# Batch 0 of an attention and gated-MLP kernel on a path of its own: k loaded channel by channel, q, x and u in two halves of the positions, in a new order of all steps

## The chip, the cores and the metric

The program runs on one core of one Trainium2 chip. Its engines work at the same time, each through its own stream of instructions: TensorE (PE in the profile; PEld is its weight load), VectorE (DVE), ScalarE (ACT), GpSimd (POOL) and SyncE (SP), which here only issues transfers. The metric is the time of one execution in device microseconds; a smaller number is better. Three runs of the kernel before gave 516.26, 516.77 and 518.28 us.

## The reference, cut to what matters

There are 8 batches, 8 heads, 576 positions and 64 channels per head. q gets a softmax over its channels, k one over its positions; k and v make a 64x64 matrix per head, q times it is x. x (576 x 512 per batch) goes through a gated MLP whose second half is mixed over the positions.

```python
q_s = softmax(q, axis=-1)                 # over 64 channels, 1e-9 in the sum
k_s = softmax(k, axis=2)                  # over 576 positions
kv  = einsum('bhsd,bhse->bhde', k_s, v)
x   = einsum('bhsd,bhde->bhse', q_s, kv)  # as (8, 576, 512)
h   = gelu_tanh(x @ w_in)                 # 512 -> 1024
u, v = h[..., :512], h[..., 512:]
v_n = (v - mean(v)) / sqrt(var(v) + 1e-6) * g_ln
v_s = einsum('ts,bsd->btd', w_sg, v_n) + b_sg[None, :, None]
out = x + (u * v_s) @ w_out
```

## The kernel before

**Steps.** All work is cut into small steps, each a function of the kernel that issues one or a few instructions (`q_max b h`, `hu_mm b f`). The text `PLAN` (line 31 on) lists some 1,400 of them by hand; the loop at line 698 calls them in that order. The class `InOrder` (line 139) chains what each of DVE, ACT, POOL and SP gets, so that every engine works strictly in the order of the plan; `mm` (line 234) does the same for PE. All four have one line in the profile, L148, and PE has L235. Between engines an instruction waits for its operands and for its buffer. All transfers are issued by SP, in the plan's order too.

**Numbers in a step's name.** The first is the batch. For q, k, kv and x the second is the half of the heads (four heads, 256 channels); for q_turn, x_high and x_low it is a pair of heads (128 channels, 0 to 3). For hu it is a block of 128 columns of the u half of w_in, for hv a tile of 128 positions. A V, A or G behind a step names the engine that it is put on.

**q.** `load_q` brings one half of the heads with channels in two groups of 32 partitions. The steps are q_max (DVE, the largest of 32 channels: 128 x 1152 to 128 x 36), q_swapm (four ACT copies of 32 partitions, which exchange the results of the two groups), q_top (DVE, the larger of both), q_sub (POOL or DVE), q_exp (ACT), q_sum, q_swapd, q_inv, q_mul (the same once more for the sum) and q_turn (DVE, a transpose in 32 x 32 pieces that gives channels on the partitions, buffers `qt`).

**k.** `load_k` brings positions on the partitions. k_ma, k_mb and k_mc (DVE) take the maximum over five tiles of positions, kt_mm (PE) transposes it, k_top (DVE) ends it, kb_mm (PE) spreads it back, k_sub (DVE, 128 x 1280) subtracts it from `kk`, k_exp is on ACT. kv_mm makes 20 products of `kk` and `vv` (a column of ones gives the sum), kv_inv and kv_scale divide into `kvt`.

**x and the MLP.** x_mm makes x on PE; x_high (ACT) rounds it to a 32-bit format that PE takes at full rate, x_low (DVE, or x_neg on PE and a copy on ACT) keeps the rest. hu_mm makes three sums of products (high by high, high by low, low by high) for one block of u, hv_mm the same for one tile of v. hv_mm 0 1 is the first product with positions as rows, and needs all of batch 0's x and four blocks of w_in. The rest (gelu, statistics, hv_norm, sg_mm, gate, out_mm, out_add, out_rest, out_store) is the same in all batches.

**Weights.** w_in and w_out come as 64-bit numbers, read as two 32-bit words. For each block of w_in wi_a (ACT) and wi_b, wi_c, wi_d (DVE, buffers `ot_i`) put the two words together, wi_h (ACT) rounds, and the rest is wi_l, on DVE, on POOL, or on PE and ACT (wi_x). hu needs blocks 0 to 3, hv blocks 4 to 7.

**Buffers.** Accumulators are three double banks (`ps2`: x, u, gate, out) and two single ones (`ps1`: kt, kb, kv, hv, wx), each taken in turn. q, k and v have two slots each (one per half of the heads), u five, `gh` and `o` four.

Of the kernel before, what the change touches and what calls it, by code (L numbers as in the profile page):

```python
# [34 lines left out]
q_top 0 1, k_sub 0 0, q_sub 0 1, wi_a 6, q_sum 0 0, q_exp 0 1, wi_b 6, k_ma 0 1, ws_h 0, wi_c 6, q_swapd 0 0, ws_x 0, k_mb 0 1, wi_d 6, ws_h 2
k_mc 0 1, q_inv 0 0, k_exp 0 0, q_sum 0 1, wi_l 1, kt_mm 0 1, wi_a 4, kv_mm 0 0, k_top 0 1, q_swapd 0 1, wi_b 4, q_mul 0 0 1 V, kb_mm 0 1, wi_h 6
load_k 1 0, ws_l 0 A, q_inv 0 1, wi_c 4, ws_h 1, kv_inv 0 0, k_sub 0 1, load_w_sg 4, q_mul 0 0 0, load_v 0 1, ws_h 3, load_w_out 0, load_g
q_mul 0 1 1, wi_a 7, k_exp 0 1, q_mul 0 1 0, q_turn 0 0, q_turn 0 1, kv_scale 0 0, load_q 1 0, q_turn 0 3, x_mm 0 0, wi_a 5, k_ma 1 0, ws_h 4, wi_b 5
q_turn 0 2, b_h, kv_mm 0 1, x_high 0 0, wi_d 4, k_mb 1 0, x_high 0 1, x_neg 0 0, load_v 1 0, load_k 1 1, wi_b 7, wi_c 5, wi_c 7, wi_x 6, wi_h 4
load_w_out 3, kv_inv 0 1, load_q 1 1, load_w_out 1, k_mc 1 0, x_low 0 0 A, x_neg 0 1, kv_scale 0 1, wi_d 5, wi_l 6 A, kt_mm 1 0, x_mm 0 1, k_top 1 0  # L40
wi_h 5, wi_d 7, load_w_out 2, x_low 0 1 A, kb_mm 1 0, q_max 1 0, wi_x 5, b_l, wi_l 4, x_high 0 3, x_high 0 2, x_low 0 3, q_swapm 1 0, x_low 0 2
k_sub 1 0, wi_h 7, wo_a 0, wi_l 5 A, wi_l 7 V, hu_mm 0 0, hu_mm 0 2, k_ma 1 1, wo_a 3, wo_b 0, k_exp 1 0, k_mb 1 1, wo_c 0, wo_b 3, wo_a 1, k_mc 1 1
q_top 1 0, wo_c 3, kt_mm 1 1, kv_mm 1 0, k_top 1 1, q_sub 1 0, q_max 1 1, kb_mm 1 1, hu_mm 0 1, load_v 2 0, load_v 1 1, q_swapm 1 1, kv_inv 1 0
kv_scale 1 0, wo_d 0, q_exp 1 0, q_top 1 1, k_sub 1 1, q_sub 1 1, wo_a 2, q_sum 1 0, hv_mm 0 1, k_exp 1 1, wo_b 2, wo_d 3, wo_b 1, q_swapd 1 0
q_exp 1 1, hv_mm 0 3, hv_gelu 0 1, wo_c 2, q_inv 1 0, wo_c 1, q_mul 1 0 0 V, q_sum 1 1, q_mul 1 0 1, hv_gelu 0 3, hv_mm 0 0, wo_d 2, q_swapd 1 1
q_turn 1 0, wo_h 2, q_inv 1 1, wo_d 1, hu_gelu 0 0, kv_mm 1 1, q_turn 1 1, q_mul 1 1 1, hu_gelu 0 2, hv_stat 0 1, hv_gelu 0 0 A, load_q 2 0
q_mul 1 1 0, x_mm 1 0, load_v 2 1, load_k 2 1, q_turn 1 3, ws_l 3, hv_mm 0 2, load_k 2 0, x_high 1 0, x_high 1 1, kv_inv 1 1, q_turn 1 2, kv_scale 1 1
x_low 1 0, load_q 2 1, hu_gelu 0 1, hv_pow 0 1, x_low 1 1, hv_sq 0 0, hv_norm 0 1, x_mm 1 1, q_max 2 0, ws_l 4, hu_mm 0 3, x_high 1 3, hv_stat 0 0 A
x_high 1 2, hv_pow 0 0, hv_gelu 0 2 A, x_low 1 3, hv_stat 0 3, hv_high 0 1, x_low 1 2, hv_pow 0 3, wo_h 3, wo_h 1, hv_mm 0 4, hv_sq 0 2, hv_low 0 1
hv_norm 0 3, ws_l 1 V, hv_high 0 3, q_swapm 2 0, hv_mm 1 1, hv_gelu 0 4 A, hv_sq 0 4, k_ma 2 0, hv_stat 0 2 A, hv_norm 0 0, k_mb 2 0, k_ma 2 1  # L50
k_mc 2 0, hv_high 0 0, hv_low 0 3, hv_pow 0 2, hv_mm 1 3, hu_gelu 0 3, q_top 2 0, hv_gelu 1 1 A, k_mb 2 1, ws_l 2 V, hv_stat 0 4 A, hv_norm 0 4
hv_pow 0 4, hv_sq 1 1, hv_norm 0 2, hv_low 0 0, hv_high 0 2, hv_mm 1 2, q_sub 2 0 V, hv_low 0 2, hv_gelu 1 3, tail_high 0, tail_again 0, tail_low 0
tail_high 1, k_mc 2 1, sg_mm 0 1, hv_gelu 1 2 A, q_max 2 1, q_exp 2 0, gate 0 1, q_swapm 2 1, hv_sq 1 2, kt_mm 2 0, kt_mm 2 1, sg_mm 0 0, k_top 2 0
tail_low 1, q_sum 2 0, q_swapd 2 0, q_top 2 1, hv_stat 1 3, wo_l 1, kb_mm 2 0, k_top 2 1, sg_mm 0 3, k_sub 2 0, q_sub 2 1, hv_stat 1 2 A, gate 0 0
k_exp 2 0, hv_pow 1 3, gate_high 0 1, q_exp 2 1, kv_mm 2 0, sg_mm 0 2, q_inv 2 0, hv_norm 1 2, hv_norm 1 3, q_mul 2 0 0 V, q_mul 2 0 1, gate_high 0 0
wo_l 2, q_sum 2 1, gate 0 3, gate_high 0 3, q_turn 2 0, wo_l 3 V, hv_mm 1 0, gate_low 0 0, q_swapd 2 1, load_k 3 0, gate 0 2, gate_low 0 1
gate_high 0 2, kv_inv 2 0, q_turn 2 1, kv_scale 2 0, wo_h 0, gate_low 0 2 G, load_q 3 0, gate_low 0 3, out_mm 0 2, wo_l 0, hv_gelu 1 0 A, kb_mm 2 1
k_sub 2 1, k_ma 3 0, out_mm 0 0, tail_again 1, hv_sq 1 0, out_add 0 2, k_mb 3 0, q_max 3 0, q_swapm 3 0, k_exp 2 1, hv_stat 1 0 A, q_inv 2 1
out_add 0 0, q_mul 2 1 0, hv_pow 1 0, q_top 3 0, hv_norm 1 0, out_mm 0 3, out_mm 0 1, q_sub 3 0 V, k_mc 3 0, out_add 0 1, out_rest 0 0 V, q_exp 3 0
kt_mm 3 0, out_rest 0 1, hu_mm 1 0, k_top 3 0, q_mul 2 1 1 V, out_add 0 3, q_sum 3 0, q_turn 2 3, hv_stat 1 1 A, kb_mm 3 0, kv_mm 2 1, hu_gelu 1 0  # L60
hv_pow 1 2, out_rest 0 2, out_rest 0 3 V, hv_pow 1 1, x_mm 2 0, load_v 3 1, out_store 0 1, hu_mm 1 3, out_store 0 3, x_high 2 0, load_k 3 1
hv_high 1 2, x_high 2 1, x_low 2 0, hv_norm 1 1, q_swapd 3 0, hv_high 1 3, hv_low 1 2, hv_high 1 0, hu_mm 1 2, hv_high 1 1, hv_low 1 3, hv_low 1 0
x_low 2 1, hu_mm 1 1, hu_gelu 1 2, hv_low 1 1, q_turn 2 2, load_q 3 1, hu_gelu 1 3, out_store 0 0, q_inv 3 0, k_sub 3 0, q_mul 3 0 0, k_ma 3 1
sg_mm 1 0, k_mb 3 1, k_mc 3 1, sg_mm 1 1, kt_mm 3 1, q_mul 3 0 1 V, q_turn 3 0, q_turn 3 1, load_v 3 0, load_q 4 0, out_store 0 2, q_max 3 1
kv_inv 2 1, q_swapm 3 1, kv_scale 2 1, hu_gelu 1 1, q_top 3 1, gate 1 0, k_exp 3 0, q_sub 3 1, sg_mm 1 2, k_top 3 1, q_max 4 0, gate_high 1 0
gate 1 1, q_swapm 4 0, gate_low 1 0 G, q_exp 3 1, kb_mm 3 1, sg_mm 1 3, gate 1 2, gate_high 1 1, q_top 4 0, q_sum 3 1, q_sub 4 0, k_sub 3 1
q_swapd 3 1, gate_low 1 1 G, k_exp 3 1, x_mm 2 1, gate 1 3, q_inv 3 1, kv_mm 3 0, gate_high 1 2, q_mul 3 1 1 V, gate_high 1 3, q_mul 3 1 0 V
kv_mm 3 1, x_high 2 2, x_high 2 3, q_turn 3 2, q_exp 4 0, load_k 4 1, gate_low 1 2, load_v 4 1, gate_low 1 3, out_mm 1 3, x_low 2 2, out_mm 1 2
kv_inv 3 0, q_turn 3 3, load_q 4 1, kv_scale 3 0, x_low 2 3, load_v 4 0, load_k 4 0, q_sum 4 0, out_add 1 3, hv_mm 2 1, q_max 4 1, out_add 1 2
out_mm 1 0, hv_gelu 2 1 A, out_rest 1 2, out_rest 1 3 V, q_swapd 4 0, k_ma 4 1, out_store 1 3, out_mm 1 1, hv_sq 2 1, out_add 1 0, q_swapm 4 1  # L70
hv_stat 2 1 A, kv_inv 3 1, hv_pow 2 1, q_top 4 1, k_ma 4 0, kv_scale 3 1, q_sub 4 1 V, x_mm 3 0, q_inv 4 0, hv_mm 2 0, q_exp 4 1, k_mb 4 0
out_add 1 1, q_mul 4 0 1, k_mb 4 1, out_rest 1 0, x_high 3 1, hv_mm 2 3, hv_gelu 2 0, out_rest 1 1 V, out_store 1 1, out_store 1 2, x_high 3 0
hv_stat 2 0, hu_mm 2 0, hv_gelu 2 3 A, hv_norm 2 0, hv_pow 2 0, q_turn 4 1, k_mc 4 1, x_low 3 0, hv_norm 2 1, hv_mm 2 2, hu_gelu 2 0, x_low 3 1
hv_sq 2 3, q_sum 4 1, k_mc 4 0, q_mul 4 0 0 V, x_mm 3 1, hu_mm 2 2, x_high 3 2, q_swapd 4 1, x_low 3 2, q_turn 4 0, hv_gelu 2 2 A, q_inv 4 1
# [673 lines left out]
```

## Time and profile before

| What | Value |
|---|---|
| Median of three runs | 516.77 us (516.26 to 518.28) |
| Span of the profiled execution | 515.9 us |
| First operation on PE | between 10 and 20 us |
| Last product on PE begins | 510.50 us |
| Last addition on DVE begins | 512.72 us |
| POOL's first operation with two operands | 15.16 us |
| Table loads on ACT | 24, 1283 ns each |

The page lists the busy time of each engine over the span, then the span in 40 slices of 12.9 us with the busy tenths of each. The table of stretches gives the same for chosen stretches, in us. A timeline row has the start, the duration, the engine, the line, the operation, and what it makes of what, with the number of like instructions that follow one another; in square brackets stands how long the engine was idle before, and which engine or transfer released it. A row of waits has the total, the number and the longest. In a row of the grouped lines the mean in ns follows the busy time. All of them come from the one profiled execution.

### The profile page before, as it was taken

To read this page: it belongs to the slowest core of one execution; us is meant where nothing else is said; L and a number is where in the kernel's file an instruction comes from. 1 tells how busy PE (TensorE), PEld (TensorE's weight loads), DVE (VectorE), ACT (ScalarE), POOL (GpSimd) and SP (SyncE) were. 2 spreads that over 40 slices of the span, in tenths; PEclk is the share of its full clock that TensorE was granted. 3 is DMA by queue.
4 is the path that set the end of the run, shared out by engine and by line. 5 is a ranking of instruction groups with operands and counts; after the bars stand their busy time and mean duration, and the time that the engine had idled before them with its cause. 6 is when DMAs were issued, how large, how long until landed. Compare 5 with 4: busy or idle time off the path is not lost.

```text
span 515.9 us, 9312 instructions
## 1 busy us (share of the span) xinstructions
PE 488.9 (95%) x3846; PEld 446.2 (86%) x3846; DVE 352.9 (68%) x597; ACT 251.1 (49%) x491; POOL 136.2 (26%) x110
## 2 busy tenths in 40 slices
PE   1659999999999999999999999999999999999996
...
DVE  6998999988887966688477866635654462266124
...
GB/s 316 361 266 243 103 246 1 53 46 99 241 10 267 48 87 6 2 75 55 192 89 56 51 243 47 1 90 118 93 1 1 55 39 1 1 0 93 1 1 91
DMA packets 19053, 48.86 MB, mean 95 GB/s; under 512 B 1602, under 2 KB 8132, under 8 KB 19012
## 3 DMA queue, kind: packets, MB, share of 16 engines
...
q8 instruction: 30, 0.49, 0.4%
q14 instruction: 11, 0.09, 0.1%
...
## 4 chain that ended last, share of the span: by engine, by line
PE 86%; DVE 9%; DMA 3%; ACT 1%; issue 1%; POOL 0%; SPq 0%
PE ps L235 86%; DMA qq<-q 2%; DVE ot_i L148 1%; DMA raw_vnh<-w_in 1%; DVE qd L148 1%; DVE kk L148 1%; DVE qm L148 1%; DVE qt L148 1%; DVE ulow L148 1%; DVE u L148 1%; DVE km L148 1%; DVE qq L148 0%; DVE o L148 0%; DVE v L148 0%; POOL ulow L148 0%
## 5 line engine op out<-in xcount | busy, mean ns | idle before, releaser
L148 POOL TENSOR_TENSOR rs<-ve,half 128x1 f32<-128x1 f32 x36 | 28.4, 788 | 113.0 <-DVE ve L148 111.7
L235 PE MATMUL ps<-ulow,wo_h 128*128 128x288 f32 x256 | 55.6, 296 | 0.9 <-DVE ulow L148 0.8
L148 DVE TENSOR_TENSOR u<-ps,u 128x576 f32<-128x576 f32 x32 | 24.0, 754 | 46.5 <-PE ps L235 41.7
L235 PE MATMUL ps<-ws_h,vnh 128*128 128x288 f32 x256 | 55.6, 299 | 0.1
L235 PE MATMUL ps<-gh,wo_h 128*128 128x288 f32 x256 | 55.7, 296 | 0.0
L235 PE MATMUL ps<-gh,wo_l 128*128 128x288 f32 x256 | 55.2, 294 | 0.0
L235 PE MATMUL ps<-ws_h,vnl 128*128 128x288 f32 x256 | 54.7, 295 | 0.0
L235 PE MATMUL ps<-ws_l,vnh 128*128 128x288 f32 x256 | 54.5, 294 | 0.0
L148 ACT CAST gh<-u 128x576 fp32r<-128x576 f32 x32 | 21.0, 670 | 57.4 <-DVE u L148 57.3
L148 POOL TENSOR_TENSOR qq<-qq,qm 128x1152 f32<-128x1152 f32 x12 | 26.1, 2176 | 78.5 <-DVE qm L148 54.4
L148 POOL TENSOR_TENSOR ulow<-u,gh 128x576 fp32r<-128x576 f32 x16 | 22.9, 1433 | 87.8 <-ACT gh L148 73.3
L148 ACT ACTIVATE v<-ps 128x512 f32<-128x512 f32 x36 | 21.6, 600 | 44.0 <-PE ps L235 37.9
L235 PEld LDWEIGHTS ps<-gh,wo_h 128*128 128x128 f32 x256 | 41.7, 188 | 1.0
L235 PEld LDWEIGHTS ps<-ulow,wo_h 128*128 128x128 f32 x256 | 41.1, 188 | 1.5 <-DVE ulow L148 1.0
L235 PEld LDWEIGHTS ps<-ws_h,vnh 128*128 128x128 f32 x256 | 40.8, 188 | 1.6 <-ACT gh L148 0.4
L235 PEld LDWEIGHTS ps<-gh,wo_l 128*128 128x128 f32 x256 | 41.3, 188 | 0.0
L235 PEld LDWEIGHTS ps<-ws_l,vnh 128*128 128x128 f32 x256 | 40.9, 188 | 0.0
L235 PEld LDWEIGHTS ps<-ws_h,vnl 128*128 128x128 f32 x256 | 40.8, 188 | 0.0
L148 DVE TENSOR_TENSOR o<-ps,x_h 128x576 f32<-128x576 f32 (+1 forms) x33 | 23.8, 728 | 24.3 <-PE ps L235 24.3
L235 PE MATMUL ps<-wi_h,x_h 128*128 128x512 f32 x144 | 40.2, 401 | 0.0
L235 PE MATMUL ps<-x_h,wi_h 128*128 128x288 f32 x256 | 40.2, 299 | 0.0
L235 PE MATMUL ps<-wi_l,x_h 128*128 128x512 f32 x144 | 39.4, 395 | 0.0
(110 smaller groups left out, 1078.6 us busy)
## 6 DMA issues: line engine op xcount, KB each, us to landing
...
out<-o SPq DMA_DIRECT2D x31, 288.0 KB, 2.5
...
```

Source lines behind the costliest of these rows:

```text
L148: ins = op(*args, **kw)
L235: tc.keep_in_program_order(nc.tensor.matmul(*args, **kw))
```

## The change

Batch 0's k comes channel by channel from a second host array: four pieces p of 128 channels by 576 positions (`load_k0`, 288 KB each, into free u slots, named `ukt` in the order). `k0_max` takes the negative maximum over the positions in one DVE reduction, `k0_exp` does the exponential with that as its bias on ACT, `k0_mm` transposes the piece in five squares on PE into a double bank, and `k0_copy` (ACT) puts it where `kv_mm` reads it. k_ma, k_mb, k_mc, kt_mm, k_top, kb_mm, k_sub and k_exp of batch 0 go. As the fifth square overlaps the fourth by 64 positions, the rows of v for the overlap are zero in batch 0.

Batch 0's q comes in two halves j of the positions (`load_q0 h j`, 288 KB); each q step runs on 18 instead of 36 columns. x0_mm, x0_high, x0_neg, x0_low, hu0_mm and hu0_gelu follow in such halves (hu0_mm: 12 products of 288 columns; the old hu_mm: 24). A swap can be put on POOL (G); all eight of batch 0 are, and twelve of later batches. wi_x now makes the rest of the blocks 0, 2, 5 and 7 (before 3, 0, 6 and 5). The whole list of steps has a new order, in which batch 0's q and k come first and the weights behind them; the last step of the program is a whole out_mm (before, the half `last_mm`). Code that wasn't called is gone.

```diff
-load_w_in 1, load_w_in 3, load_w_in 0, load_w_in 2, load_q 0 0, load_eye, load_k 0 0, load_q 0 1, load_w_in 6, wi_a 1, load_w_sg 2, load_w_sg 1
...
+load_q0 1 0, q0_max 1 0, load_q0 0 0, q0_max 0 0, load_k0 3, q0_swapm 1 0 G, q0_top 1 0, q0_sub 1 0, load_k0 0, k0_max 3, k0_exp 3, q0_exp 1 0
+k0_max 0, load_q0 1 1, q0_max 1 1, q0_swapm 0 0 G, q0_top 0 0, q0_sub 0 0, q0_sum 1 0, load_q0 0 1, q0_max 0 1, load_k0 2, k0_max 2, load_b, b_h
+q0_swapd 1 0 G, q0_inv 1 0, q0_exp 0 0, q0_sum 0 0, load_eye, q0_swapm 0 1 G, q0_top 0 1, load_w_in 3, wi_a 3, wi_b 3, k0_exp 2, q0_mul 1 0, load_k0 1
...
+    def k0_max(p):
+        V.tensor_reduce(out=top0(p), in_=kt0(p), axis=AX.X, op=ALU.max, negate=True)
+
+    def k0_exp(p):
+        A.activation(kt0(p), kt0(p), AF.Exp, bias=top0(p))
+
+    def k0_mm(p):
+        ps, t = flat(bank(ps2, "k0", p)), kt0(p)
+        for i in range(5):
+            c = min(i * P, S - P)
+            mm(ps[:, i * P:i * P + P], t[:, c:c + P], eye, is_transpose=True, start=True, stop=True)
+
+    def k0_copy(p, E=A):
+        kk, a = kk_s(0, p // 2, at=p // 2), p % 2
+        to, of = kk[:, :, a * P:a * P + P], flat(st["k0", p])[:, 0:5 * P].rearrange("p (t c) -> p t c", t=5)
...
+    def rows_of(b, h, j=None):
+        t = qq_s(b, h, at=h).rearrange("p a j c -> p (a j) c")
+        return t if j is None else t[:, 18 * j:18 * j + 18]
...
-    def swap(dst, src):
+    def swap(E, dst, src):
         for i in range(4):
-            A.copy(out=dst[i * 32:i * 32 + 32], in_=src[(i ^ 1) * 32:(i ^ 1) * 32 + 32])
+            to, of = dst[i * 32:i * 32 + 32], src[(i ^ 1) * 32:(i ^ 1) * 32 + 32]
+            if E is A:
+                A.copy(out=to, in_=of)
+            else:
+                E.tensor_copy(out=to, in_=of)
...
+    def q_swapm(b, h, E=A, j=None):
+        swap(E, stat(qs_s, b, h, j), stat(qm_s, b, h, j))
...
+    def x0_mm(h, j):
+        ps = bank(ps2, "x0", h, j)
+        for z in range(2):
+            for a in range(2):
+                zs, cs = slice(z * D, z * D + D), slice(a * D, a * D + D)
+                mm(ps[cs, z, 0:HS], kvt_s(0, h)[zs, a], qt_s(0, 2 * h + a)[zs, j * HS:j * HS + HS], start=True, stop=True)
...
+    def hu0_mm(f, j):
+        ps, fs, m = bank(ps2, "u0", f, j), slice(f * P, f * P + P), 0
+        for w, x in ((wi_h, x_h), (wi_l, x_h), (wi_h, x_l)):
+            for c in range(4):
+                mm(ps[:, j, 0:HS], w[:, c, fs], x(0)[:, c, j * HS:j * HS + HS], start=m == 0, stop=m == 11)
+                m += 1
...
+    arr["k0"] = np.ascontiguousarray(k[0].transpose(0, 2, 1)).reshape(NP, P, S)
...
+    vs[0, S:] = vs[0, ST * P:S]
+    vs[0, ST * P:S] = 0
```

Where the order moves work is seen in the instructions of each engine. First POOL, from its first work of the plan on, before. `qq` is q, `qm` its maxima, `qd` its sums, `qs` and `qe` their swapped copies; the instruction called ISA prepares POOL and computes nothing.

```order
L148 ISA
L148 TENSOR_TENSOR qq_0_98<-qq_0_98,qm_0_143 128x1152
L148 TENSOR_TENSOR qq_1_103<-qq_1_103,qm_1_164 128x1152
L148 TENSOR_TENSOR wi_l<-ot_i_106,wi_h 128x4x128
L148 TENSOR_TENSOR qq_0_98<-qq_0_98,qd_0_187 128x576
L148 TENSOR_TENSOR qq_1_103<-qq_1_103,qd_1_211 128x576 x2
```

The same place of the changed kernel:

```order
L149 COPY qs_1_103<-qm_1_95 32x18 x4
L149 ISA
L149 TENSOR_TENSOR qq_1_93<-qq_1_93,qm_1_95 128x576
L149 COPY qs_0_119<-qm_0_99 32x18 x4
L149 TENSOR_TENSOR qq_0_97<-qq_0_97,qm_0_99 128x576
L149 COPY qe_1_137<-qd_1_126 32x18 x4
L149 COPY qs_0_119<-qm_0_99 32x18 x4
L149 TENSOR_TENSOR qq_1_93<-qq_1_93,qd_1_126 128x576
L149 COPY qs_1_103<-qm_1_95 32x18 x4
L149 COPY qe_0_188<-qd_0_145 32x18 x4
```

The copies are new on POOL, and the first four of them stand ahead of the ISA instruction, with the subtraction and the second swap behind it.

DVE, its first instructions behind five memsets, before (`ot_i` are the words of w_in, `km` the maxima of k):

```order
L148 TENSOR_SCALAR ot_i_106<-ot_i_106 128x512
L148 SCALAR_TENSOR_TENSOR ot_i_106<-raw_vnh,ot_i_106 128x512 x2
L148 TENSOR_SCALAR ot_i_119<-ot_i_119 128x512
L148 SCALAR_TENSOR_TENSOR ot_i_119<-raw_vnl,ot_i_119 128x512
L148 TENSOR_SCALAR ot_i_128<-ot_i_128 128x512
L148 SCALAR_TENSOR_TENSOR ot_i_119<-raw_vnl,ot_i_119 128x512
L148 SCALAR_TENSOR_TENSOR ot_i_128<-raw_vnh,ot_i_128 128x512
L148 TENSOR_SCALAR ot_i_135<-ot_i_135 128x512
```

And in the changed kernel (`k0m` are the maxima of batch 0's k):

```order
L149 TENSOR_REDUCE qm_1_95<-qq_1_93 128x18
L149 TENSOR_REDUCE qm_0_99<-qq_0_97 128x18
L149 TENSOR_TENSOR qm_1_95<-qm_1_95,qs_1_103 128x18
L149 TENSOR_REDUCE k0m<-ukt_101 128x1
L149 TENSOR_REDUCE k0m<-ukt_110 128x1
L149 TENSOR_REDUCE qm_1_95<-qq_1_93 128x18
L149 TENSOR_TENSOR qm_0_99<-qm_0_99,qs_0_119 128x18
L149 TENSOR_REDUCE qd_1_126<-qq_1_93 128x18
L149 TENSOR_REDUCE qm_0_99<-qq_0_97 128x18
L149 TENSOR_REDUCE k0m<-ukt_130 128x1
L149 SCALAR_TENSOR_TENSOR qd_1_126<-qd_1_126,qe_1_137 128x18
```

The weights, which led, now stand from the fifteenth instruction behind the memsets on; the seventh, a maximum of 18 columns, reads what the second swap on POOL makes.

PE, from its first product on, before (`eye` is the identity, `minus` its negative):

```order
L235 MATMUL ps_0_79<-ot_i_119,eye 128x512
L235 MATMUL ps_0_79<-wi_h,minus 128x512
L235 MATMUL ps_1_80<-ot_i_128,eye 128x512
L235 MATMUL ps_1_80<-wi_h,minus 128x512
L235 MATMUL ps_0_79<-eye,km_0_155 128x128 x2
L235 MATMUL ps_1_80<-eye,kt_0_171 128x128 x2
L235 MATMUL ps_0_76<-ghws_121,eye 128x320
```

And in the changed kernel:

```order
L235 MATMUL ps_0_75<-eye,ukt_110 128x128 x5
L235 MATMUL ps_1_76<-eye,ukt_159 128x128 x5
L235 MATMUL ps_2_77<-eye,ukt_130 128x128 x5
L235 MATMUL ps_0_75<-eye,ukt_101 128x128 x5
L235 MATMUL ps_0_78<-vv_1_207,kk_1_210 64x65 x20
L235 MATMUL ps_1_79<-vv_0_212,kk_0_184 64x65 x20
L235 MATMUL ps_1_76<-qt_2_172,kvt_1_277 64x288
L235 MATMUL ps_1_76<-qt_3_177,kvt_1_277 64x288
```

PE now turns k first and makes both kv products and a part of x; the first product on a weight comes behind the third and fourth of these on `qt`.

More of the change, by code (lines that the diff above doesn't have):

```diff
@@ L35 @@
[L35 to L74, printed above, removed]
@@ new lines @@
+q0_sub 0 1, k0_mm 3, k0_copy 3, q0_exp 0 1, load_w_in 2, q0_sum 0 1, k0_copy 1, load_w_in 5, wi_d 1, load_w_in 7, q0_exp 1 1, kv_mm 0 1, kv_mm 0 0
+kv_inv 0 1, q0_mul 0 0, wi_h 1, wi_d 0, kv_scale 0 1, load_w_in 4, x0_mm 1 0, neg, kv_inv 0 0, wi_a 2, q0_sum 1 1, q0_swapd 0 1 G, wi_b 2, wi_h 0
+wi_x 0, wi_h 3, q0_inv 0 1, x0_high 1 0, x0_neg 1 0, wi_l 1, load_w_sg 3, load_k 1 0, wi_c 2, wi_l 3, wi_a 7, wi_a 5, kv_scale 0 0, q0_mul 0 1
+q0_turn 0 0, q0_turn 1 0, wi_d 2, x0_mm 0 0, wi_h 2, q0_turn 1 1, wi_x 2, x0_high 0 0, x0_neg 0 0, wi_b 5, q0_swapd 1 1 G, x0_low 1 0 A, load_k 1 1
```

280 lines of the change are left out of this document (172 added, 108 removed).

## The prediction

> **What bounds the kernel now.** I read the page first.
>
> ```profile
> span 515.9 us, 9312 instructions
> ...
> PE 488.9 (95%) x3846; PEld 446.2 (86%) x3846; DVE 352.9 (68%) x597; ACT 251.1 (49%) x491; POOL 136.2 (26%) x110
> ...
> PE   1659999999999999999999999999999999999996
> ...
> DVE  6998999988887966688477866635654462266124
> ```
>
> TensorE (PE) is busy at nine tenths or more in every slice but the first three and the last. So the span is a head in which PE starves, and then one unbroken stream of products. The table of stretches shows who starves it (columns: start, end and length in us; busy us of PE, PEld, DVE, ACT, POOL; granted clock; DMA share; GB/s).
>
> ```profile
> 10.00:20.00 10.00, 5.49 (x11) 2.50 (x11) 9.97 (x16) 7.29 (x18) 4.10 (x2) 0.99 1.03 396
> 20.00:30.00 10.00, 6.53 (x50) 4.03 (x50) 9.90 (x20) 9.01 (x18) 4.67 (x5) 0.66 0.72 243
> 30.00:40.00 10.00, 7.12 (x61) 4.60 (x62) 9.69 (x18) 5.83 (x10) 4.00 (x4) 0.51 1.00 330
> 40.00:50.00 10.00, 10.00 (x76) 8.46 (x75) 8.87 (x15) 7.80 (x15) 0.68 (x1) 0.98 0.75 268
> ```
>
> From 10 to 40 us DVE is busy 97 to 100%, PE 55 to 71% and partly at half clock (0.66, 0.51). PE's waits, longest last column, name the same engine.
>
> ```profile
> PE ps L235 <- DVE ot_i L148: 11.4, 1, 11.4
> PE ps L235 <- DVE kvt L148: 4.1, 1, 4.1
> ```
>
> PE's own timeline (start, duration) gives the head's end and a landmark.
>
> ```profile
> 25.01 2.15 PE L235 MATMUL ps<-vv,kk 128*64 128x65 f32 x40
> ...
> 38.09 1.91 PE L235 MATMUL ps<-ot_i,eye 128*128 128x512 f32 x2
> ...
> 40.22 0.49 PE L235 MATMUL ps<-x_h,minus 128*128 128x288 f32 x2
> ...
> 40.87 1.20 PE L235 MATMUL ps<-qt,kvt 64*64 64x288 f32 x16
> ...
> 42.27 1.02 PE L235 MATMUL ps<-ot_i,eye 128*128 128x512 f32 x2
> ...
> 43.36 1.23 PE L235 MATMUL ps<-x_h,wi_h 128*128 128x288 f32 x8
> ...
> 46.54 1.23 PE L235 MATMUL ps<-x_h,wi_h 128*128 128x288 f32 x8
> ...
> 50.03 1.39 PE L235 MATMUL ps<-vv,kk 128*64 128x65 f32 x40
> ...
> 54.82 1.10 PE L235 MATMUL ps<-wi_h,x_h 128*128 128x512 f32 x4
> ```
>
> At 43.36 the first large product begins (hu_mm 0 0; one costs 46.54 - 43.36 = 3.18), and PE hardly stops again. At 54.82 the first token-major product begins (hv_mm 0 1). What PE has left behind that point is the same work in both kernels, except that there the changed one still owes half of a hu product (1.59), where the old one owes a whole. So **the break-even start of hv_mm 0 1 in the changed kernel is 54.82 + 1.59 = 56.41**, and the change is worth what its head does to that start, plus any new stall in the stream.
>
> **The change part by part.**
>
> *Removed for batch 0:* k_ma, k_mb, k_mc, k_top and k_sub on DVE and k_exp on ACT, for both halves of heads. *Added:* four reductions, four ACT exponentials, 20 transposes on PE, four ACT copies back. The rows (mean ns behind the busy us):
>
> ```profile
> L148 DVE TENSOR_TENSOR kk<-kk,ps 128x1280 f32<-128x1280 f32 x16 | 23.4, 1476 | 4.8 <-PE ps L235 4.8
> L148 ACT ACTIVATE kk<-kk 128x1280 f32<-128x1280 f32 x16 | 20.4, 1274 | 5.0 <-DVE kk L148 4.7
> L148 DVE TENSOR_REDUCE qm<-qq 128x36 f32<-128x1152 f32 x16 | 21.5, 1344 | 8.7 <-DMA qq<-q 8.7
> L148 DVE STREAM_TRANSPOSE qt<-qq 128x576 f32<-128x576 f32 x32 | 24.2, 765 | 3.1 <-POOL qq L148 1.7 <-PE ps L235 1.3
> ```
>
> A reduction over 576 values is half of the 1344 ns row, about 0.65, so the four cost 2.6 where two k_sub alone cost 3.0; PE pays more (20 transposes of 128 columns for 8), but in time in which it waits. The q steps in halves cost DVE the same elements in twice the instructions.
>
> *Moved:* the weights. In the old order DVE works on w_in from 4.87 on; in the new one it starts on batch 0's q and k, and the four weight blocks that the first products need (3, 1, 0, 2) follow behind. And *POOL takes the four swaps of 32-row pieces* that ACT did; nothing on POOL precedes the first one. Its rows:
>
> ```profile
> 0.34 0.10 POOL L734 MEMSET const-uint8-127<- 128x1 uint8 x1
> 15.16 2.26 POOL L148 TENSOR_TENSOR qq<-qq,qm 128x1152 f32<-128x1152 f32 x1 [14.72 <-DVE qm L148]
> ...
> 35.84 1.34 POOL L148 TENSOR_TENSOR wi_l<-ot_i,wi_h 128x512 fp32r<-128x512 f32 x1 [0.40 <-ACT wi_h L148]
> ...
> 71.61 0.56 POOL L148 TENSOR_TENSOR rs<-ve,half 128x1 f32<-128x1 f32 x1 [1.96 <-DVE ve L148]
> ```
>
> ```profile
> L148 ACT COPY qs<-qm 32x36 f32<-32x36 f32 x64 | 14.0, 219 | 37.2 <-DVE qm L148 36.5
> ```
>
> No row shows a small POOL copy. Bounds: 0.10 (its memset) to 0.56 (its smallest two-operand row); ACT's copy, the nearest in kind, is 0.22. I take 0.2, so **0.8 a swap**.
>
> POOL's program has a second thing with no row: one instruction ("ISA" in the order) ahead of its first two-operand operation, which can only prepare POOL for such work. In the old order it is POOL's first step and has all of the 14.72 us of idle time before 15.16 to itself; in the new one it stands *behind* the first four copies, which wait for the first reduction. What it costs is between 0 and 14.7; the row is an idle time, near to neither end, and I take the middle, **7 us, in the open**. The Trainium skill, "GPSIMD Engine Reference", section "2.1 Instruction dispatch", says that the first call of newly loaded POOL code pays a load of about 6 us that has no instruction in the profile; by it the sum would come out 1 us lower, and no row of this trace shows it.
>
> *The head of the new order, as a sum.* DVE's cost of one instruction is its row less the 0.09 by which neighbours overlap (10.43 to 10.76 is 0.33 for a row of 0.42). The last four rows are for what follows the steps.
>
> ```profile
> 2.33 1.11 DVE L148 MEMSET vn<- 1x512 f32 x2 [0.16 <-DVE vn L148]
> ...
> 10.43 0.42 DVE L148 TENSOR_SCALAR ot_i<-ot_i 128x512 uint32<-128x512 uint32 x1
> 10.76 0.69 DVE L148 SCALAR_TENSOR_TENSOR ot_i<-raw_vnh,ot_i 128x512 uint32<-128x512 uint32 x1
> ...
> 14.55 0.43 DVE L148 TENSOR_TENSOR km<-km 128x256 f32<-128x256 f32 x1
> ...
> 20.66 1.15 DVE L148 TENSOR_SCALAR ot_i<-ot_i 128x512 uint32<-128x512 uint32 x1
> ...
> 34.64 1.08 DVE L148 TENSOR_TENSOR km<-km 128x256 f32<-128x256 f32 x1
> ...
> 35.97 1.75 DVE L148 SCALAR_TENSOR_TENSOR ot_i<-raw_wo_h,ot_i 128x512 uint32<-128x512 uint32 x1
> ```
>
> 1. DVE's memsets end at 3.44; the first reduction, behind its 288 KB load, at about 4.4.
> 2. POOL: swap to 5.3, preparation to 12.3, q0_sub 1 0 (half of 2.26) to 13.4, the swap of the other half of heads to 14.3. Only then can DVE do q0_top 0 0, at **14.4**. DVE's order is fixed: having done two more k0_max and a q0_max by 7.5, it stands there, and behind it q0_sum 1 0, k0_max 2 and the first weight step (wi_b 3), for which ACT's exponential, PE's transposes and PE's first wi_x wait.
> 3. From there to the end of wi_d 2, DVE does 7 reductions (4.6), four weight blocks at 0.33 + 0.60 + 0.60 (6.1), 3 q0_inv (about 0.47 each, 1.4), 4 q0_turn (half of 765 ns, 1.5), kv_inv and kv_scale twice (1.1) and 3 maxima (0.3): 15.0, and waits some 2.0 for POOL's swaps and for the two kv products, which PE makes at half clock (2.15 each): **31.4**.
> 4. wi_h 2 on ACT (0.6 with its hand-over), wi_x 2 on PE at half clock (40.22 - 38.09 = 2.13), x0_neg: the first hu0_mm at **34.8**.
> 5. PE to hv_mm 0 1: seven half products (11.1), two wi_x at full clock (43.36 - 42.27 = 1.09 each), two x0_mm (1.2, as one x_mm at 40.87), x0_neg, the transposes of batch 1, ws_x and a kv product (1.39), together 3.8: 18.3, so **53.1**.
>
> A sum of undisturbed rows is too short, and the last three rows above say by how much: 20.66 is a form that takes 0.42 elsewhere, 34.64 one of 0.43 (14.55), 35.97 one of 0.69, so they lost 0.7, 0.65 and 1.05, 2.4 together, each beside a POOL operation (one is quoted, 35.84 to 37.18). The new head has about as much two-operand work on POOL (four subtractions, four products, three more: some 14 us beside the 12.8 that the table of stretches has from 10 to 40). With 2.4 the new start is 55.5, **0.9 ahead of the break-even 56.41**.
>
> The Trainium skill, "SBUF — State Buffer", section "SBUF: two separate sides", says that DVE and POOL share a port pair as an exclusive lock, the loser blocking fully. The trace agrees in those three rows (1.75 beside 0.69). The rule speaks against this change, as POOL's copies would take the lock too; if each of the eight swaps cost DVE 0.2, the sum would be 1.6 worse.
>
> *Behind the head.* The order of all later steps is new, DVE (68% over the span) and ACT (49%) have slack there, and loads stand ahead of their uses by about what they take, the closest being v of batch 1 (issued some 6.6 us ahead). ACT has four more table loads:
>
> ```profile
> L148 ACT ACT_TABLE_LOAD x24 | 30.8, 1283 | 9.9 <-PE ps L235 8.8 <-PEq L734 0.7
> ```
>
> At 1.28 each they are hidden while ACT has slack, else they cost up to 5.1. PE has 1.7 us more work over the kernel (12 transposes, halves of x_neg), all within the head sum. I take 1.2 for stalls behind the head, between 0 and 5. The last step is now a whole out_mm instead of a half: one larger store against one more pair of adds.
>
> ```profile
> out<-o SPq DMA_DIRECT2D x31, 288.0 KB, 2.5
> ...
> out<-o SPq DMA_DIRECT2D x2, 144.0 KB, 1.8
> ```
>
> That is +0.7 for the store and about as much less on DVE, so nothing. **The sum: -0.9 + 1.2 = +0.3** on the span of 515.9. The three runs lie 0.4 to 2.4 above that span, their median 0.87 above, and I keep that distance: 517.1.
>
> **The rivals.**
>
> *The preparation costs nothing* (or POOL does it while it waits for the first reduction). Then q0_top 0 0 comes near 7.4, but DVE's work and the loads fill part of the 7 us, and the sum gives the first hu0_mm at 28.2: 6.6 earlier. That is **510.5**. For it: the trace has no row for the instruction, and the releaser of POOL's first operation at 15.16 is DVE's qm, its operand. Against: with 14.7 us of idle time ahead of it, that start proves nothing.
>
> *POOL's opening is dearer* (slower than before). The place is POOL between q0_max 1 0 and DVE's q0_top 0 0, and then the chain of eight swaps that DVE's halves wait for. If a copy costs what the 0.56 row does, a swap is 2.24, and five of them in the chain are 1.44 longer each: +7.2 in the head, less the 1.2 of stalls behind, which a later head covers, so 517.1 + 6.0 = **523.1**. The time passes 516.8 + 2.6 when the head is 3.5 later: from 0.37 us a copy on (5 swaps of 4 copies, each 0.175 over my 0.2). A preparation of 14.7 instead of 7 gives about the same, 523.6, and passes that point from 10.5 on. For it: ACT takes 0.22 already, and the only small row of POOL is 0.56. Against: in the halves a copy moves half of the elements of ACT's, and has no second operand to fetch.
>
> *The new order stalls PE later:* the four table loads or a late load cost up to 5 instead of 1.2: about **521**. Against it: DVE's slices behind the head are mostly at four to eight tenths.
>
> That the change doesn't do what it says is no rival of weight: the order shows each instruction in its place.
>
> **How the numbers follow.** About 0.5% (2.6 us) is what a measurement here can tell from no change. Chances: the forecast (preparation of 4 to 10 us, 0.2 a copy) 0.40; no preparation to be seen 0.32; POOL's opening dearer 0.23; later stalls 0.05. The range takes the first two with their spread and the third up to about 523: 509.5 to 523. Within the forecast's own spread (514 to 520) some 0.05 falls below -2.6 and 0.06 above +2.6. Faster: 0.30 of the second case and 0.05 = 0.35. Slower: 0.18 of the third, 0.05 of the last and 0.06 = 0.29. Same: the rest, 0.36. Signs are mixed, so the likeliest case decides the time: 517.1.
>
> **What would show it.** In POOL's timeline: a gap between the first copy of qs and the first subtraction of 128x576 (7 expected, 0 for the first rival), and the duration of a copy (0.2; 0.56 for the second). In DVE's: idle time before the second small maximum (about 7), gapless work after it. In PE's: first hu0_mm (x_h,wi_h x4) near 36 to 37, first wi_h,x_h product near 55, no stall over 1 us behind. I am wrong if DVE isn't gapless from 14 to 31, if the kv products or the loads of k come later than 25, or if waits of PE beyond 60 us add up to more than 5.

## The result and the profile after

The changed kernel takes 522.94 us (median of four runs, 521.73 to 523.98), the kernel before 517.13 on the same chip (four runs, 516.26 to 518.28): 1.0116 times as long, with a 95% interval of 1.0092 to 1.0139. The forecast was no change, 517.1. The profiled execution took 523.98 us for a span of 522.2; it is the slowest of the four, and the difference of the two profiles (6.3 us) is 0.5 larger than that of the medians (5.8).

The page of the changed kernel, the lines that answer to those shown of before:

```profile
span 522.2 us, 9404 instructions
...
PE 491.4 (94%) x3862; PEld 447.4 (86%) x3862; DVE 355.9 (68%) x596; ACT 245.0 (47%) x445; POOL 166.7 (32%) x199
...
PE   0788899999999999999999999999999999999996
...
DVE  7999999779764876669567755567875673453234
```

By the page's slices of 13 us the head hardly got shorter: the first seven of PE read 0, 7, 8, 8, 8, 9, 9, where the old page has 1, 6, 5, 9, 9, 9, 9. Two slices are fuller and three thinner, and what is lost later is spread too thinly to show in them. The table of stretches shows the head (columns as before):

```profile
10.00:20.00 10.00, 6.52 (x74) 5.66 (x75) 9.93 (x18) 7.36 (x12) 8.61 (x19) 1.00 1.04 361
20.00:30.00 10.00, 5.81 (x58) 2.97 (x54) 9.54 (x24) 6.29 (x13) 7.00 (x11) 0.92 1.00 354
30.00:40.00 10.00, 10.00 (x68) 7.87 (x68) 8.41 (x15) 8.02 (x15) 5.28 (x7) 0.91 0.78 255
40.00:50.00 10.00, 10.00 (x97) 8.86 (x96) 9.97 (x15) 7.47 (x11) 5.42 (x6) 1.00 0.81 273
50.00:60.00 10.00, 8.11 (x71) 6.11 (x69) 9.86 (x15) 8.49 (x15) 7.73 (x10) 1.00 0.39 133
```

PE is full from 30 us on, ten us earlier than before, but not full any more from 50 to 60, with DVE at 99%. POOL is busy 8.61 and 7.00 us from 10 to 30 us, where it had 4.10 and 4.67. The landmarks on PE's timeline, and the first operations on POOL's:

```profile
31.51 0.85 PE L235 MATMUL ps<-x_h,wi_h 128*128 128x288 f32 x4
...
52.38 1.17 PE L235 MATMUL ps<-wi_h,x_h 128*128 128x512 f32 x4 [1.54 <-DVE kk L149]
```

```profile
4.45 0.89 POOL L149 COPY qs<-qm 32x18 f32<-32x18 f32 x4 [4.01 <-DVE qm L149]
5.64 1.16 POOL L149 TENSOR_TENSOR qq<-qq,qm 128x576 f32<-128x576 f32 x1 [0.29 <-DVE qm L149]
```

POOL's subtraction follows its four copies after 0.29 us, and that is the wait for DVE's q_top: the preparation of POOL, forecast at 7 us, costs nothing that can be seen. The first four copies take 0.89 as forecast (0.8). hv_mm 0 1 starts at 52.38, **4.0 us ahead of the break-even 56.41**. So 4.0 + 6.3 = 10.3 us were lost behind it. PE's waits from 45 us on (engine and tile waited for, total, number, longest), the seven longest of the changed kernel and all of the kernel before:

```profile
PE ps L235 <- DVE kk L149: 1.5, 1, 1.5
PE ps L235 <- DVE qt L149: 1.5, 1, 1.5
PE ps L235 <- DVE x_l L149: 1.2, 2, 0.8
PE ps L235 <- DVE ulow L149: 1.1, 1, 1.1
PE ps L235 <- DVE vn L149: 0.9, 1, 0.9
PE ps L235 <- ACT v L149: 0.8, 2, 0.5
PE ps L235 <- DVE vnl L149: 0.7, 2, 0.4
```

```profile
PE ps L235 <- DVE ulow L148: 0.8, 1, 0.8
PE ps L235 <- POOL ulow L148: 0.2, 1, 0.2
```

All but one of the seven are waits for DVE; before, there was one for DVE and a shorter one for POOL.

To see when time is lost, a running number helps: the time t, plus the sum of the normal start-to-start distances (medians of the trace of before) of all that PE still has to do at t. While PE works at its normal pace it stands still; it rises by what PE loses. Worked out from the PE rows of each trace, for the kernels that tell most (e1 to e9 are the experiments below):

| t in us | before | after | e1 | e3 | e6 | e8 | e9 |
|---|---|---|---|---|---|---|---|
| 45 | 503.3 | 497.6 | 503.3 | 497.8 | 496.0 | 496.1 | 497.5 |
| 95 | 504.3 | 504.5 | 504.3 | 505.8 | 498.7 | 501.0 | 504.5 |
| 200 | 507.3 | 511.5 | 512.0 | 509.1 | 504.3 | 506.8 | 509.7 |
| 480 | 510.5 | 517.0 | 517.6 | 513.1 | 510.0 | 512.3 | 515.2 |

Before and after: **a lead of 5.7 us at 45 us, gone at 95, and a further 6.3 lost from there to the end** (12.5 where the old order loses 6.2). Each of the two losses got a theory.

### The profile page after: what moved, and what is told of

Read it like the earlier page. It is cut to its first block, busy times and chain, and to the rows that moved or that the text cites. A ratio compares the mean times of both kernels' runs of the same rounds, so it can differ in the third digit from the quotient of the medians.

```text
span 522.2 us, 9404 instructions
## 1 busy us (share of the span) xinstructions
PE 491.4 (94%) x3862; PEld 447.4 (86%) x3862; DVE 355.9 (68%) x596; ACT 245.0 (47%) x445; POOL 166.7 (32%) x199
## 4 chain that ended last, share of the span: by engine, by line
PE 71%; DVE 16%; ACT 5%; DMA 4%; issue 1%; POOL 1%; SPq 1%; ACTq 0%; DVEq 0%; POOLq 0%
PE ps L235 71%; DVE qd L149 3%; DVE ot_i L149 2%; DMA raw_x_l<-w_out 2%; DVE km L149 1%; DVE v L149 1%; DVE qt L149 1%; DMA kk<-k 1%; DVE o L149 1%; DVE ot_o L149 1%; DVE vnl L149 1%; DMA ukt<-k 1%; DVE kk L149 1%; DVE qm L149 1%; ACT v L149 1%
## 5 line engine op out<-in xcount | busy, mean ns | idle before, releaser
L149 ACT ACTIVATE u<-ps 128x576 f32<-128x576 f32 (+1 forms) x36 | 21.2, 599 | 62.3 <-PE ps L235 62.0
L235 PE MATMUL ps<-x_h,wi_h 128*128 128x288 f32 x256 | 41.8, 303 | 0.8 <-DVE x_l L149 0.8
L235 PEld LDWEIGHTS ps<-x_h,wi_h 128*128 128x128 f32 x256 | 36.0, 190 | 5.0 <-DVE x_l L149 1.7
## 6 DMA issues: line engine op xcount, KB each, us to landing
raw_vnl<-w_in SPq DMA_DIRECT2D x2, 512.0 KB, 4.7
```

What stands on the lines that cost most here:

```text
L149: ins = op(*args, **kw)
L235: tc.keep_in_program_order(nc.tensor.matmul(*args, **kw))
```

## The experiments

Theory 1 is on the second loss: the new list of the steps behind batch 0 costs about 6 us by itself. Theory 2 is on the first: DVE is the bound up to about 95 us, and in the new head POOL holds it up, so that the lead is only borrowed. All kernels are built from the changed one's code and differ in the list of steps alone; where the old k path is used, the rows of v stand as before. The kernel before, run beside each, took 516.62 to 517.23 us, so the times can be compared.

**e1, the old head and the new tail.**

```diff
 (old order up to) q_turn 2 1, kv_scale 2 0, wo_h 0, gate_low 0 2 G, load_q 3 0, gate_low 0 3
-out_mm 0 2, wo_l 0, hv_gelu 1 0 A, kb_mm 2 1, k_sub 2 1, k_ma 3 0
+hv_stat 1 1 A, hv_gelu 1 0 A, kb_mm 2 1, hv_norm 1 1, k_sub 2 1, k_exp 2 1
 (and the rest of the new order)
```

> The old order of steps up to the first out_mm of batch 0, the changed order behind it (with its POOL swaps). Theory 1 (the order of the steps behind batch 0 loses about 6 us by itself: PE waits at 165, 184, 188, 228 and 324 us that the old order hasn't): about 522 to 523 us, as slow as the whole change, with waits of PE of 3 to 6 us behind 110 us. Rival (those waits are left over from the new head, whose POOL work delayed DVE): 516 to 518 us, no wait of PE over 0.5 us behind 110.

Measured: 524.98 us, 1.015 of before (1.0119 to 1.0182). PE's timeline of e1, its waits from 160 to 192 us:

```profile
167.43 0.54 PE L232 MATMUL ps<-ulow,wo_h 128*128 128x288 f32 x2 [1.07 <-DVE ulow L146]
...
185.84 1.32 PE L232 MATMUL ps<-x_h,wi_h 128*128 128x288 f32 x8 [0.80 <-DVE x_l L146]
...
189.96 1.20 PE L232 MATMUL ps<-qt,kvt 64*64 64x288 f32 x16 [0.46 <-DVE x_l L146]
```

These are the changed kernel's waits (1.06 at 166.72, 0.78 at 185.16, 0.45 at 189.28), at the same steps and of the same size, though the head is the old one. Theory 1 holds: from 95 us on e1 loses 13.3, the changed kernel 12.5, the old order 6.2. (Two waits of e1, 1.5 and 1.0 us, lie at the seam, around 105 and 110 us; the time is 2 us above the expected 522 to 523.)

The new list differs from the old one not only in its order. It also puts some steps on other engines: behind 100 us, 15 products of q stand on POOL in the changed kernel and 10 before, among the new ones both `q_mul 3 1`, which the old list has on DVE. How much of the 6 us is the order, and how much this choice of engines, e1 can't tell; e9 below bears on it.

**e2, the new head and the old tail.**

```diff
 (new order up to) hv_norm 1 2, hv_high 1 2, out_mm 0 2, out_mm 0 3, hv_low 1 2, load_v 3 1
-hv_high 1 1, kt_mm 3 0, q_mul 2 1 0, out_add 0 3, hu_mm 1 1, hu_gelu 1 1
+load_q 3 0, out_add 0 2, q_max 3 0, q_swapm 3 0, q_mul 2 1 0, q_top 3 0
 (and the rest of the old order)
```

> The changed order up to a few steps behind batch 0's out_mm, the old order behind it (swaps on ACT there). Theory 1: about 516 to 518 us, as the lead of the new head is gone by 95 us and the old tail adds no waits. Rival: about 522 to 523.

Measured: 527.8 us, 1.0202 (1.0169 to 1.0236), against both. A single new wait of e2 makes most of it, from 123.8 to 130.3 us:

```profile
PE ps L235 <- DVE kt L149: 6.7, 2, 6.5
```

At the seam batch 3's k steps come late for where the old order has their products. A spliced list has a seam with a price of its own; e2 says nothing on theory 1.

**e3, the new head up to hv_mm 0 1, the old order from there.**

```diff
 (new order up to) wi_l 6, wi_l 4, wo_a 3, kv_inv 1 0, wo_a 0, hu0_mm 1 1
-hv_mm 0 1, q_inv 1 0, kv_scale 1 0, wo_b 3, wo_c 3, q_swapd 1 1 G
+ws_h 2, ws_h 1, ws_h 3, ws_h 4, wo_b 0, wo_c 0, wo_b 3, wo_c 3, load_v 2 0, load_v 1 1, kv_scale 1 0, wo_d 0, wo_a 2, hv_mm 0 1
 (and the rest of the old order)
```

> The changed order only up to the first token-major product (hv_mm 0 1), the old order from there. It starts 4 us ahead of the break-even at that product. Theory 2 (the lead is eaten between 50 and 95 us because DVE is the bound there and was held up some 8 us by POOL's operations on q in the new head): PE waits again some 4 to 6 us between 50 and 110, end at 515 to 518. Rival (the changed order between 50 and 110 us is what eats it): the lead stays, 511 to 513.

Measured: 520.59 us, 1.0059 (1.004 to 1.0078), above both expected times. The lead is gone here too at 95: the running number rises by 8.0 from 45 us on, and then by 7.3, near the old order's 6.2. So another order of the stretch didn't keep the lead. Its seam wait (2.8 us for kvt, the scaled kv product) is part of the 8.0, so this alone doesn't settle theory 2.

**e4, all swaps on ACT.**

```diff
-q0_swapm 1 0 G, q0_swapm 0 0 G, q0_swapd 1 0 G
+q0_swapm 1 0, q0_swapm 0 0, q0_swapd 1 0
...
-q_swapm 1 0 G, q_swapm 1 1 G, q_swapd 1 1 G
+q_swapm 1 0, q_swapm 1 1, q_swapd 1 1
 (and the other swaps on POOL, twenty in all)
```

> The whole change, but all twenty swaps on ACT in place of POOL, at the same places of the order. The prediction's slower rival (POOL's swaps are what costs): faster by 2 us or more than the changed kernel, 521 or less. Against it, a POOL swap took 0.89 us in the trace where ACT's took 0.92, and the rows in which DVE is held up stand beside POOL's two-operand work: then 522 to 524, within 0.3% of the changed kernel.

Measured: 536.87 us, 1.0381 (1.0352 to 1.041): neither. Up to 100 us the running number is that of the changed kernel within 0.5 us, so in the head it makes no difference to PE which engine does the swaps; the prediction's slower rival falls. The 14 us come behind: ACT works in the order of the list, and a swap placed for POOL makes ACT wait for DVE with all that stands behind it. ACT's waits for the maxima and sums of q add up to 35.6 us, for 23.9 in the changed kernel. The longest new wait, on PE:

```profile
PE ps L235 <- DVE u L149: 5.1, 1, 5.1
```

**e6, no subtraction and product of q on POOL for batches 0 and 1.**

```diff
-q0_sub 1 0, q0_sub 0 0, q0_mul 1 0, q0_sub 1 1, q0_mul 0 0
-q_sub 1 0, q_sub 1 1, q_mul 1 0 1
 (and the others of batches 0 and 1, 14 steps in all)
```

> The whole change, but q_sub and q_mul of batches 0 and 1 are left out (subtraction of the maximum and division by the sum; 14 operations of POOL in the first 62 us). Theory 2 (these operations hold DVE up by some 8 to 10 us in the first 60 us, and that eats the lead): DVE's held-up time before 60 us falls from 12 to 4 us or less, the waits of PE between 50 and 95 us fall from 6 to 2 or less, and the time to 516 to 519. Rival (DVE's own work is the bound whether it is held up or not): 521 to 523.

Measured: 516.8 us, 0.9991 of before (0.9977 to 1.0005). What POOL does to DVE is seen where both timelines are laid side by side. DVE's, then POOL's, of the changed kernel:

```profile
17.00 1.41 DVE L149 SCALAR_TENSOR_TENSOR ot_i<-raw_vnl,ot_i 128x512 uint32<-128x512 uint32 x1
18.34 1.38 DVE L149 TENSOR_SCALAR ot_i<-ot_i 128x512 uint32<-128x512 uint32 x1
...
45.32 1.93 DVE L149 SCALAR_TENSOR_TENSOR ot_i<-raw_wo_h,ot_i 128x512 uint32<-128x512 uint32 x1
...
47.62 3.22 DVE L149 SCALAR_TENSOR_TENSOR ot_i<-raw_wo_l,ot_i 128x512 uint32<-128x512 uint32 x2
```

```profile
15.47 2.39 POOL L149 TENSOR_TENSOR qq<-qq,qm 128x576 f32<-128x576 f32 x2
17.83 1.61 POOL L149 TENSOR_TENSOR qq<-qq,qd 128x576 f32<-128x576 f32 x1
...
44.57 2.13 POOL L149 TENSOR_TENSOR qq<-qq,qm 128x1152 f32<-128x1152 f32 x1
47.78 2.51 POOL L149 TENSOR_TENSOR qq<-qq,qm 128x1152 f32<-128x1152 f32 x1 [1.07 <-DVE qm L149]
```

Forms of 0.69 and 0.42 us take 1.41, 1.38, 1.93 and 1.6 each beside a POOL operation on q. Summed over DVE's rows of the first 60 us (what each takes over the tenth percentile of its form, where POOL has an operation beside it) that is 12.3 us in the changed kernel and 4.1 before; of it 10.1 and 1.3 beside POOL's q_sub and q_mul. Without these, in e6, it is 2.3, and the waits for kk and qt are gone. Of e6's waits from 45 us on, three lie before 95 us (vn 0.22, one of the two for v 0.32, kt 0.22), all others behind 120:

```profile
PE ps L234 <- DVE x_l L148: 1.2, 2, 0.8
PE ps L234 <- DVE ulow L148: 1.1, 1, 1.1
PE ps L234 <- ACT v L148: 0.8, 2, 0.5
PE ps L234 <- DVE vnl L148: 0.7, 2, 0.4
PE ps L234 <- DVE vn L148: 0.2, 1, 0.2
```

The lead at 95 us is 5.6 now, and from there to the end e6 loses 11.3, like the other kernels in the new order. Of the 6.1 us that e6 gains over the changed kernel, 5.8 are there at 95 us. Leaving the steps out also shortens the chains of q, which this run can't part from the hold-up.

**e7, the same operations on DVE.**

```diff
-q0_sub 1 0, q0_mul 1 0, q_sub 1 0, q_mul 1 0 1
+q0_sub 1 0 V, q0_mul 1 0 V, q_sub 1 0 V, q_mul 1 0 1 V
 (and so for the same 14 steps)
```

> The whole change, but q_sub and q_mul of batches 0 and 1 are on DVE in place of POOL. Theory 2: DVE's rows are no longer held up there (12 us to 3 or less), but it has some 11 us of work more, so the time stays within 2 us of the changed kernel, 521 to 525. Rival (POOL's work hides beside DVE's): 530 or more.

Measured: 524.58 us, 1.0142 (1.0121 to 1.0162). The held-up time falls to 1.7 us, but DVE has the work itself, and nothing is won. On POOL these operations are not free: there they hold DVE up by about as much (10.1 us) as their work takes on DVE (11.6).

**e8, without DVE's steps on w_out.**

```diff
-wo_b 1, wo_b 3, wo_c 3, wo_b 0, wo_c 1, wo_d 1, wo_c 0, wo_d 0, wo_b 2, wo_d 3, wo_c 2, wo_d 2
```

> The whole change, but DVE's twelve steps that put w_out's words together (wo_b, wo_c, wo_d, some 6.2 us between 33 and 72 us) are left out; ACT's and POOL's steps on w_out stay. If DVE is the bound between 45 and 95 us: the waits of PE there (6 us) fall to 2 or less, and the time by 3 to 6, 517 to 520; the waits behind 160 us stay as they are. Rival (the waits there come from single late steps of the new order, not from DVE's load): 521 to 523.

Measured: 519.52 us, 1.0048 (1.0033 to 1.0063), 3.4 us less than the changed kernel for 6.2 us of DVE's work. At 95 us the lead is 3.3, and the waits behind 160 us are unchanged (ulow 1.1, x_l 1.2). PE's waits from 45 to 100 us shrink from 4.8 to 2.3 us, not quite to the 2 or less expected. So DVE's load is what bounds this stretch, at least in part: 6.2 us less work gave 3.4.

**e9, batch 3's second half of q on DVE.**

```diff
-q_sub 3 1, q_mul 3 1 0, q_mul 3 1 1
+q_sub 3 1 V, q_mul 3 1 0 V, q_mul 3 1 1 V
```

> The whole change, but q_sub and both q_mul of batch 3's second half of heads are on DVE in place of POOL; in the changed kernel they stand on POOL at 164 and 181 us, where DVE's ulow row took 2.67 us in place of 0.75 and its two km rows 2.50 in place of 0.9, just ahead of PE's waits for ulow (1.23) and x_l (0.94 and 0.62). If being held up by POOL makes these waits too: the wait at 165 goes and those at 184 and 188 shrink, 1.2 to 2.8 us faster than the changed kernel, 520 to 521.7. Rival (the order alone makes them late): they stay, 522.5 to 523.5.

In its trace DVE's ulow row is whole again, and the waits at 165 and 184 us are gone; the one at 188 grew from 0.62 to 1.50 against the normal distance, as DVE now does two products of 0.7 us itself ahead of it. DVE's row:

```profile
163.87 0.76 DVE L149 TENSOR_TENSOR ulow<-u,gh 128x576 fp32r<-128x576 f32 x1 [0.52 <-POOL ulow L149]
```

In the changed kernel this row takes 2.67 us beside POOL's subtraction of q (163.91, 2.13 us long). So these two waits, too, were made by POOL holding DVE up. The time doesn't show it: 522.88 us, 1.0108 (1.0092 to 1.0125), where the running number has 1.8 us less. But this trace is of e9's fastest run (522.46) and that of the changed kernel of its slowest (523.98), which is 1.5 of the 1.8, so the size of the gain stays open.

**e5, e10 and e11, parts of the change in the old order.**

```diff
 e5
-load_k 0 0, k_ma 0 0, k_mb 0 0, kt_mm 0 0, kb_mm 0 0, k_sub 0 0, k_exp 0 0
+load_k0 0, load_k0 1, k0_max 0, k0_max 1, k0_exp 0, k0_exp 1, k0_mm 0, k0_mm 1, k0_copy 0, k0_copy 1
 e10, as e5, and
-q_swapm 0 0, q_swapm 0 1, q_swapd 0 0, q_swapd 0 1
+q_swapm 0 0 G, q_swapm 0 1 G, q_swapd 0 0 G, q_swapd 0 1 G
-load_k 1 0, load_v 0 1
+load_v 0 1, load_k 1 0
 (and so for the rest of both lists of steps)
 e11, the old order and k path
-q_swapm 0 0, q_swapm 0 1, q_swapd 0 0, q_swapd 0 1
+q_swapm 0 0 G, q_swapm 0 1 G, q_swapd 0 0 G, q_swapd 0 1 G
```

> The old order of all steps; only batch 0's k goes channel by channel (k0_max, k0_exp, k0_mm, k0_copy at the places of k_ma to k_exp), q and x whole, swaps on ACT. Theory (the k path saves DVE about 3 us in the stretch where DVE is the bound, and the old order behind it adds no waits): 512 to 515 us, hv_mm 0 1 some 2 to 4 us earlier than 54.8. Rival (ACT, which gets 2.7 us more, or the lead is eaten before 100 us as in the whole change): 516 to 518.

> As the run with k by channel alone in the old order, but batch 0's four swaps on POOL, and the load of v's second half ahead of that of batch 1's k. That run had ACT busy 98% from 20 to 30 us, and PE waited for ACT (3.7 us for ukt, ws_h and kk), for the two waits behind a late w_in block (2.4) and for v (2.0). If ACT's load and the v load were what ate the k path's saving on DVE: hv_mm 0 1 near 52 to 54 us and 513 to 516 us. Rival (nothing is to be had from the k path in this order): 517 to 519.

> The old order and k path, only batch 0's four swaps on POOL in place of ACT. Theory (the old head is bound by DVE; a POOL swap takes as long as ACT's): 515.5 to 518, same as before within 0.3%. Rival (ACT's queue is a bound in the head): 514 or less.

Measured: e5 518.51 us (1.0034, 1.0017 to 1.0051), e10 518.78 (1.0033, 1.0021 to 1.0044), e11 521.68 (1.0082, 1.0065 to 1.0099). None is faster than before, and e10 lies where its rival had it. In e5's profiled execution, the slowest of ten (521.32), DVE is relieved (8.14 of ten us from 20 to 30, where it had 9.90), but ACT, with the exponentials and copies in two pieces each, becomes the engine that ends most waits of PE in the head; it is busy 9.77:

```profile
20.00:30.00 10.00, 7.58 (x61) 5.62 (x61) 8.14 (x14) 9.77 (x20) 4.01 (x4) 0.66 0.71 225
```

e10 relieves ACT again (8.06 of ten us), and its running number is that of before at 45 us (503.1): the saving of the k path isn't seen. e11 missed both expectations. Beside a busy DVE a swap on POOL isn't 0.9 us long:

```profile
14.65 2.18 POOL L146 COPY qs<-qm 32x36 f32<-32x36 f32 x4 [14.21 <-DVE qm L146]
```

One block of w_in also arrived 2.4 us later in e11's trace (8.07 for 5.62), with the same loads ahead of it, so not all of its 4.5 us need be the swaps'.

**e12 and e13, batch 2 later.**

```diff
 e12
-hv_pow 0 4, hv_gelu 1 3, q_max 2 1, k_ma 2 1, hv_norm 0 2, ws_l 2, hv_mm 1 2, q_max 2 0
+hv_pow 0 4, hv_gelu 1 3, hv_norm 0 2, ws_l 2, hv_mm 1 2
...
+gate 0 0, hv_sq 1 2, sg_mm 0 2, q_max 2 1, k_ma 2 1, wo_l 1, gate 0 2, q_max 2 0
 e13, as e12, and
-q_sub 3 1, q_mul 3 1 0, q_mul 3 1 1
+q_sub 3 1 V, q_mul 3 1 0 V, q_mul 3 1 1 V
```

> The whole change, but batch 2's steps on q, k and kv, with the loads that follow them, stand 40 steps later in the order (less and less so towards x_mm 2 0): some 8 us of DVE's work then come behind batch 0's gates in place of ahead of them. If DVE's queue up to batch 0's out_mm is the bound between 45 and 105 us: the waits for vn, km and kt at 89 to 96 us (1.9 us together) go, out_mm of batch 0 starts 2 us or more earlier than 109.9, and the time falls by 1.5 to 4, 519 to 521.5. Rival (the work is only moved, the waits come back at batch 2's kv or x): 522 to 524.

> Both edits together: batch 2's steps 40 places later, and q_sub and q_mul of batch 3's second half of heads on DVE. If the waits at 165 to 189 us add to the loss in the new order: 1 to 2 us faster than with batch 2 later alone. Rival (they are made up for behind): equal within 0.1%.

Measured: 540.34 us (1.0457, 1.0442 to 1.0471) and 539.83 (1.0451, 1.0429 to 1.0473). The first half of e12's expectation came true: there is no wait from 65 to 104 us, and the running number at 100 is 503.2 for 505.6. Then PE stands for batch 2's k:

```profile
PE ps L235 <- DVE kt L149: 8.1, 2, 5.9
PE ps L235 <- DVE vnl L149: 3.4, 3, 1.8
PE ps L235 <- DVE km L149: 3.3, 3, 2.9
```

The work was only moved, and 40 places were far too many. e13 lies 0.5 us below e12 with overlapping intervals, so it doesn't size the waits at 165 to 189 us either.

## Why the prediction was wrong

1. **The bound and the landmark were right as far as they went.** The head did end earlier, and hv_mm 0 1 came 4.0 us ahead of the break-even.
2. **The preparation of POOL, 7 us in the open, was wrong:** 0; no load of POOL code is to be seen either. The first rival had the mechanism, with hv_mm 0 1 some 7.5 us ahead. It came 4.0 ahead. The likely reason is that DVE was held up more: 8 us more than before in the first 60 us (12.3 for 4.1), and by the same measure some 7 us for 3 in the first 40, where the sum allows 2.4. That allowance was taken from the old head, on the ground that POOL's two-operand work is about as much; up to 40 us it is (15.4 us for 12.8), but now more of it lies beside operations of DVE that it stops. The two kv products, put at 2.15 us each, were too dear (2.82 together).
3. **The step that failed is "I take 1.2 for stalls behind the head, between 0 and 5".** Measured: 10.3, by the two profiles. The prediction took the stream behind hv_mm 0 1 as the same work and so the same time, and had slack on DVE there. But the page that it shows has DVE at nine tenths from 52 to 103 us, and in the old trace's stretches DVE is at 93, 99 and 98% while PE is never idle:

```profile
40.00:60.00 20.00, 20.00 (x165) 17.36 (x165) 18.62 (x32) 15.61 (x29) 6.06 (x3) 0.99 0.57 201
60.00:80.00 20.00, 20.00 (x153) 15.73 (x152) 19.79 (x43) 15.48 (x42) 9.48 (x8) 1.00 0.44 159
80.00:100.00 20.00, 20.00 (x168) 18.91 (x167) 19.64 (x28) 14.62 (x30) 8.20 (x6) 1.00 0.07 16
```

PE ran there without a wait because DVE was just in time. A PE that is 5.7 us earlier meets a DVE that isn't. Shown by e6 and e8: take from DVE what holds it up, or work, and the lead stays to that extent. The prediction's own sign came true: PE's waits beyond 60 us add up to 6.4 us, more than 5.
4. **The new list behind batch 0, a rival at 0.05 with up to 5 us, costs about 6** (12.5 for 6.2 from 95 us on). e1 shows it with the old head, and e3 shows the old tail near its old price behind a new head. Four waits of it, all for DVE (vnl at 127, ulow at 165, x_l at 184 and 189), make 3.4 us over the normal distances; none is for a load or a table load, which the rival named. In two of the four e9 shows POOL's work on q as the cause. The rest is in pieces under 0.7 us, whose causes were not traced.
5. **The slower rival named the wrong place.** Batch 0's swaps cost 0.89 to 1.61 us on POOL, 0.85 on ACT (e4), not 2.24, and moving them to ACT changes nothing for PE up to 100 us. The result lies at its time (523.1), and so at the edge of the range, by chance.
6. The sum closes: -5.7 at 45 us, +5.9 up to 95, +6.3 behind make +6.5; the spans differ by 6.3, the medians by 5.8.

What stays open: how much of the hold-up and how much of the shorter chains makes e6's gain, how much of the 6 us behind 95 us is the order and how much the choice of engines, and what the two waits of e9 are worth in time. No version was found that beats the kernel before.

The Trainium skill, "SBUF — State Buffer", section "SBUF: two separate sides", has a shared port pair that a POOL operation, or a DVE operation with two inputs from SBUF or in a mode that takes both ports, holds for its whole length, while the other is blocked fully. The rows at 17.00 and 45.32 us agree: each ends 0.55 us behind the POOL operation beside it, so that nearly all of its undisturbed 0.69 us lies behind that operation's end. So does e9's row at 163.87, where the block is gone with the POOL operation (0.76 for 2.67).
